# Norms' partition sums on GpSimd for three of four batches, in a fused attention and gated-FFN kernel

## The chip, the cores and the metric

One core of one Trainium2 chip. The metric is the device time of one execution in microseconds. All times below are medians of several executions.

## The reference

Four batches of cross-covariance attention over channels, and on its output a gated feed-forward block. N = 5824 rows, C = 256 channels, F = 1024.

```python
qn = q / (np.linalg.norm(q, axis=1, keepdims=True) + 1e-06)    # norms over the rows, one per channel
kn = k / (np.linalg.norm(k, axis=1, keepdims=True) + 1e-06)
s = kn.transpose(0, 2, 1) @ qn / tau                           # 256 x 256 per batch
s = s - s.max(-1, keepdims=True)
a = np.exp(s); a /= a.sum(-1, keepdims=True) + 1e-09
x = (v @ a).reshape(B * N, C)
out = ((x @ w1) * (x @ w2)) @ w3 @ w_out
```

## The kernel before

The kernel folds `a` into `w1` and `w2` (tiles `Wf`) and `w3 @ w_out` into `W_sb`. Each batch is then a long stream of steps: two products `a` and `b` from `vT` and `Wf` (TensorE), a cast `as` of `a` to bf16 (ScalarE), a product `abs` = `as` x `b` (VectorE), and the output product `o` (TensorE). Eight steps make a chunk of 512 rows, twelve chunks a batch; the last chunk of a batch is small, 192 rows. After each chunk `o` is copied out of PSUM (`osb`) by ScalarE and VectorE. The `a` and `b` products of all steps, and the row sums and folds too, rotate through four PSUM buffers with the tag `ab`:

```python
t = psum.tile([P, 512], F32, tag="ab", name=f"{'ab'[w]}_{b}_{c}_{j}", bufs=4)
...                                                       # 2 matmuls each
nc.scalar.copy(a_sb[:, :n], tiles[0][:, :n])              # the cast `as`
nc.vector.tensor_mul(ab, a_sb, tiles[1])                  # `abs`
```

While one batch streams, the softmax of the next one is prepared in between. Each engine's instructions run in the order in which they are issued here (below, casts stand 1.31 us behind exponentials that wait); an agenda of times (estimates of the program's own clock, not device times) decides where each piece falls:

```python
def norms():                                  # sums of squares of q and k, per partition
    a1 = work.tile([P, 2, C], F32, tag="acc1", ...)
    nc.vector.tensor_add(a1, accs[n][:, 0], accs[n][:, 1])
    st["ksq"] = a1[:, 1, :]; st["qsq"] = a1[:, 0, :]
def k_row():                                  # the chain: sum over partitions, then 1/(sqrt + eps)
    m = psum.tile([P, 512], F32, tag="ab", name=f"row_{n}", bufs=4)
    nc.tensor.matmul(m[:, :C], lhsT=ones_pp, rhs=st["ksq"], start=True, stop=True)
    nc.scalar.activation(out=kr, in_=m[:, :C], func=AF.Ln)
    ...                                       # three more on kr
def q_sums():
    ...                                       # two matmuls into ss_{n}, then q_norm: two small ScalarE, two small VectorE
def scaled():                                 # G is k^T q; s = G * kr on VectorE, then e = exp(s * r) on ScalarE
    for ct in range(CT): scale(ct)
    exps()
def sums(): ...                               # row sums of e on TensorE, into an "ab" buffer
...
head = [(0.0, norms), (0.5, k_row), (0.4, q_sums)]
return head + [(0.0, scaled), (0.2, sums)] + [(0.43, lambda i=i: fold(i)) for i in range(8)]
...
# times of: norms, k_row, q_sums, scaled, sums, then eight folds
ts = [t1 + 1.0, t1 + 3.5, t1 + 4.0, t1 + 8.0, t1 + 12.0] + [t1 + 13.0 + 0.9 * i for i in range(8)]
```

Of the kernel before, what the change touches and what calls it, by code (L numbers as in the profile page):

```python
# [7 lines left out]


# [1 line left out]
AF = mybir.ActivationFunctionType  # L11
ALU = mybir.AluOpType
F32 = DT.float32
# [11 lines left out]
def kernel(  # L25
# [213 lines left out]
    def soft_units(n):  # L239
        st = {}  # L240

        def k_first():
            d = work.tile([P, CT, P], F32, tag="sq", name="dk", bufs=2)
            nc.vector.tensor_mul(d, S["k"], ident.unsqueeze(1).to_broadcast([P, CT, P]))
            st["ksq"] = d.rearrange("p c t -> p (c t)")

        def q_first():
            d = work.tile([P, CT, P], F32, tag="sq", name="dq", bufs=2)
            ss = work.tile([P, CT], F32, tag="ss0", name="ss0", bufs=1)
            for ct in range(CT):  # L250
                nc.vector.tensor_tensor_reduce(
                    out=d[:, ct, :], in0=S["q"][:, ct, :], in1=ident, scale=1.0, scalar=0.0,
                    op0=ALU.mult, op1=ALU.add, accum_out=ss[:, ct : ct + 1],
                )
            st["ss"] = ss

        def scaled_first():
            scale(0)
            q_norm(st["ss"])
            scale(1)  # L260
            exps()

        def norms():
            a1 = work.tile([P, 2, C], F32, tag="acc1", name=f"acc1_{n}", bufs=1)
            nc.vector.tensor_add(a1, accs[n][:, 0], accs[n][:, 1])
            st["ksq"] = a1[:, 1, :]
            st["qsq"] = a1[:, 0, :]

        def k_row():

            m = psum.tile([P, 512], F32, tag="ab", name=f"row_{n}", bufs=4)
            nc.tensor.matmul(m[:, :C], lhsT=ones_pp, rhs=st["ksq"], start=True, stop=True)  # L272
            kr = work.tile([P, C], F32, tag="kr", name=f"kr_{n}", bufs=1)
            nc.scalar.activation(out=kr, in_=m[:, :C], func=AF.Ln)  # L274
            nc.scalar.activation(out=kr, in_=kr, func=AF.Exp, scale=0.5)
            nc.scalar.activation(out=kr, in_=kr, func=AF.Ln, bias=eps_t)  # L276
            nc.scalar.activation(out=kr, in_=kr, func=AF.Exp, scale=-1.0)
            st["kr"] = kr

        def q_sums():  # L280
            m = psum.tile([P, 512], F32, tag="ab", name=f"ss_{n}", bufs=4)
            for ct in range(CT):
                nc.tensor.matmul(
                    m[:, ct : ct + 1], lhsT=st["qsq"][:, ct * P : (ct + 1) * P], rhs=ones_f,
                    start=(ct == 0), stop=(ct == CT - 1), skip_group_check=True,
                )
            q_norm(m[:, :CT])

        def q_norm(src):
            r = work.tile([P, CT], F32, tag="r", name=f"r_{n}", bufs=2)  # L290
            nc.scalar.activation(out=r, in_=src, func=AF.Ln)
            nc.scalar.activation(out=r, in_=r, func=AF.Exp, scale=0.5)
            nc.vector.tensor_scalar_add(r, r, 1e-6)
            nc.vector.reciprocal(r, r)
            if inv_tau != 1.0:
                nc.vector.tensor_scalar_mul(r, r, inv_tau)
            st["r"] = r

        def scale(ct):
            if ct == 0:  # L300
                st["s"] = work.tile([P, CT, C], F32, tag="s", name=f"s_{n}", bufs=1)
            nc.vector.tensor_mul(st["s"][:, ct, :], G_tiles[n][:, ct, :], st["kr"])

        def exps():
            e = work.tile([P, CT, C], BF16, tag="e", name=f"e_{n}", bufs=2)
            for ct in range(CT):
                nc.scalar.activation(
                    out=e[:, ct, :], in_=st["s"][:, ct, :], func=AF.Exp, scale=st["r"][:, ct : ct + 1]
                )
            st["e"] = e  # L310

        def scaled():
            for ct in range(CT):
                scale(ct)
            exps()

        def sum_mm(c2):
            if c2 == 0:
                st["sum"] = psum.tile([P, 512], F32, tag="out" if n == 0 else "ab", name=f"sum_{n}", bufs=3 if n == 0 else 4)
                Wf[n] = wf_pool.tile([P, CT, 2, F], BF16, tag="Wf", name=f"Wf_{n}")  # L320
            m = st["sum"]
            for c1 in range(CT):
                nc.tensor.matmul(
                    m[:, c1 : c1 + 1], lhsT=st["e"][:, c2, c1 * P : (c1 + 1) * P], rhs=ones_b,
                    start=(c1 == 0 and c2 == 0), stop=(c1 == CT - 1 and c2 == CT - 1), skip_group_check=True,
                )
            if c2 == CT - 1:
                rs = work.tile([P, CT], F32, tag="rs", name=f"rs_{n}", bufs=2)
                nc.vector.tensor_scalar_add(rs, m[:, :CT], 1e-9)
                nc.vector.reciprocal(rs, rs)  # L330
                st["rs"] = rs

        def sums():
            sum_mm(0)
            sum_mm(1)

        def fold_mm(i, c2, tag="ab", on_act=None):
            h, rest = divmod(i, 4)
            w, c1 = divmod(rest, 2)
            if c2 == 0:  # L340
                st["fold", i] = psum.tile(
                    [P, 512], F32, tag=tag, name=f"fold_{n}_{i}", bufs={"ab": 4, "out": 3}[tag]
                )
            nc.tensor.matmul(  # L344
                st["fold", i], lhsT=st["e"][:, c2, c1 * P : (c1 + 1) * P], rhs=w12[:, c2, w, h * 512 : (h + 1) * 512],
                start=(c2 == 0), stop=(c2 == CT - 1),
            )
            if c2 == CT - 1:
                dst = Wf[n][:, c1, w, h * 512 : (h + 1) * 512]
                if on_act if on_act is not None else i % 2 == 0:  # L350
                    nc.scalar.activation(out=dst, in_=st["fold", i], func=AF.Copy, scale=st["rs"][:, c1 : c1 + 1])  # L351
                else:
                    nc.vector.tensor_scalar_mul(dst, st["fold", i], st["rs"][:, c1 : c1 + 1])

        def fold(i, tag="ab", on_act=None):
            fold_mm(i, 0, tag)
            fold_mm(i, 1, tag, i % 2 == 0 if on_act is None else on_act)

        def first_folds():
            sum_mm(0)  # L360
            fold_mm(0, 0)
            fold_mm(1, 0)
            sum_mm(1)
            fold_mm(0, 1)
            fold_mm(1, 1)
            fold(2)
            transpose_half_on_pe(0, 0, 0, False)
            fold(3, on_act=True)
            fold(4, "out", on_act=False)
            fold(5, "out")  # L370

        if n == 0:
            return [k_first, k_row, q_first, scaled_first, first_folds] + [lambda i=i: fold(i) for i in range(6, 8)]
        head = [(0.0, norms), (0.5, k_row), (0.4, q_sums)]
        return head + [(0.0, scaled), (0.2, sums)] + [(0.43, lambda i=i: fold(i)) for i in range(8)]


# [12 lines left out]
    def at(t, cost, fn):  # L390
        seq[0] += 1
        agenda.append((t, seq[0], cost, fn))
# [106 lines left out]
    busy(14)  # L499
    load_piece("k", 0, 0, (half,))  # L500
    load_piece("q", 0, 0, (half,))
    masks.make_identity(nc, ident)
    nc.vector.tensor_copy(ident_b, ident)
    w3_wout = vT_pool.tile([P, (NT - 1) * C], BF16, tag="vT", name="w3_wout")
    w3_bf = w3_wout[:, : FT * F].rearrange("p (j l) -> p j l", l=F)
    wout_sb = w3_wout[:, FT * F : FT * (F + D)].rearrange("p (l d) -> p l d", d=D)
# [2 lines left out]
    def transpose_w3():  # L509

        for h in range(FT // 2):
            m = in_pool.tile([P, 2, FT, P], BF16, tag="k", name=f"w3T_{h}", bufs=IN_BUFS["k"])
            nc.sync.dma_start_transpose(m, w3_bf[:, 2 * h : 2 * h + 2, :])
            w3T.append(m)

    w3r = moe_w3.rearrange("(jh jl) l -> jl jh l", jl=P)
    w1r = moe_w1.rearrange("(ch cl) f -> cl ch f", cl=P)
# [54 lines left out]
    def w_unit(jt):  # L572
# [10 lines left out]
        if jt == FT - 1:  # L583
            w_ready[0] = True


    def make_agenda(b):
        agenda.clear()
# [2 lines left out]
        if b == 0:  # L591
            for i in range(2):
                at(1.5 + 0.6 * i, 0.43, soft0[5 + i])
            at(4.0, 0.5, lambda: transpose_half_on_pe(0, 0, 1, False))
            at(7.0, 0.5, lambda: transpose_half_on_pe(0, 1, 0, True))
            at(8.0, 0.5, lambda: transpose_half_on_pe(0, 1, 1, False))
# [4 lines left out]
            moves = [("v", 0, 3, 29.0), ("qk", 1, 0, 38.0), ("qk", 1, 1, 43.0), ("v", 0, 4, 50.0), ("qk", 1, 2, 58.0)]  # L601
            moves += [("qk", 1, 3, 63.0), ("v", 0, 5, 70.0), ("qk", 1, 4, 81.0), ("qk", 1, 5, 87.0)]
            moves += [("v", 1, 0, 96.0), ("v", 1, 1, 106.0), ("v", 1, 2, 116.0), ("qk", 2, 0, 126.0)]
            t0, t1 = 58.0, 120.0
        else:
            moves = [("v", b, 3, 1.0), ("qk", n, 1, 10.0), ("qk", n, 2, 17.0), ("v", b, 4, 26.0), ("qk", n, 3, 38.0)]
            moves += [("v", b, 5, 46.0), ("qk", n, 4, 58.0), ("qk", n, 5, 66.0)]
# [20 lines left out]
        for i, (cst, fn) in enumerate(units):  # L628
            at(t0 + (t1 - t0) * i / len(units), cst, fn)
        soft = soft_units(n)  # L630
        ts = [t1 + 1.0, t1 + 3.5, t1 + 4.0, t1 + 8.0, t1 + 12.0] + [t1 + 13.0 + 0.9 * i for i in range(8)]
        for t, (cst, fn) in zip(ts, soft):
            at(t, cst, fn)
        agenda.sort()
# [50 lines left out]
```

## Time and profile before

| | before |
|---|---|
| time, median | 575.47 us in the runs given at the start; 575.46 to 575.79 in the rounds below |
| span of the profiled run | 573.6 us |
| TensorE busy | 561.9 us, 98% |
| next busiest: VectorE, ScalarE | 65%, 59% |

These are lines of the timeline of before around batch three's exponentials, ScalarE, then VectorE, then TensorE. Columns: start, duration, engine, line, operation, output<-inputs, shapes, count; in brackets the idle time just before it and what ended it.

```profile
295.28 0.58 ACT L431 CAST as<-a 128x512 bf16<-128x512 f32 x1 [0.35 <-PE a L425]
296.96 0.91 ACT L307 ACTIVATE e<-s,r 128x256 bf16<-128x256 f32 x2 [1.09 <-DVE s L302]
297.77 1.05 ACT L431 CAST as<-a 128x512 bf16<-128x512 f32 x2
...
296.50 0.75 DVE L302 TENSOR_TENSOR s<-G,kr 128x256 f32<-128x256 f32 x2
...
299.41 0.60 PE L466 MATMUL o<-W_sb,abs 128*128 128x256 bf16 x4
299.85 0.24 PE L323 MATMUL sum<-ones_b,e 128*128 128x1 bf16 x4
```

ScalarE already stands idle for 1.09 us here, with the exponentials at the head of its queue and casts behind them. TensorE does not notice: `sum` follows `o` without a bracket. How close that is can be worked out. TensorE starts an `a` every 1.30 us, so with four buffers for two products a step, the buffer of an `a` is wanted again two steps, 2.60 us, later. The first cast behind the exponentials serves the `a` that started at 295.95; its buffer is wanted at 298.55, and the cast, half of the 1.05 us from 297.77, ends at about 298.3. That leaves some 0.25 us.

### The profile page before, as it was taken

How to read it: one execution, taken by the hardware profiler on the slowest of the kernel's cores; microseconds unless marked ns; L12 is line 12 of the kernel's file. 1: busy time of each engine (PE TensorE's matmuls, PEld its weight loads, DVE VectorE, ACT ScalarE, POOL GpSimd, SP SyncE). 2: the span in 40 equal slices, each digit the busy share in tenths (PEclk: the TensorE clock that was granted, in tenths of full speed). 3: DMA queues.
4: the chain of work that ended last, by engine and by line, in shares of the span. 5: the costliest groups of instructions: out<-in, count | busy, mean ns of one | idle time of the engine just before them, and what ended most of it. 6: DMA issues, size and time to landing. Idle time of an engine off the chain costs nothing.

```text
span 573.6 us, 10125 instructions
## 1 busy us (share of the span) xinstructions
PE 561.9 (98%) x3760; PEld 357.0 (62%) x3766; DVE 374.1 (65%) x597; ACT 337.9 (59%) x624; POOL 71.0 (12%) x162
## 2 busy tenths in 40 slices
PE   8789999999999999999999999999999999999997
PEld 4755576776666666666666666666665666666665
DVE  0047744787967567887776567778876656565564
ACT  0046534777766567776765567767765555454453
POOL 5240020202010111221000012021100000000000
PEclk9999999999999999999999999999999999999999
DMA  8999959779574696495661596675740325221011
GB/s 163 211 194 208 188 99 235 175 171 213 134 185 108 123 207 151 95 190 120 147 147 49 117 192 143 132 142 119 184 110 38 85 74 146 63 63 74 38 71 59
DMA packets 74561, 76.93 MB, mean 134 GB/s; under 512 B 54161, under 2 KB 58257, under 8 KB 74513
## 3 DMA queue, kind: packets, MB, share of 16 engines
q0 software_dynamic: 15504, 39.46, 39.2%
q1 hardware_dynamic: 58784, 36.64, 21.1%
q8 instruction: 29, 0.48, 0.3%
q10 hardware_dynamic: 224, 0.20, 0.1%
q14 instruction: 20, 0.16, 0.1%
HBM read 78.91 MB, written 23.86 MB: 179 GB/s over the span
## 4 chain that ended last, share of the span: by engine, by line
PE 91%; DMA 5%; ACT 1%; issue 1%; DVE 1%; POOL 1%; ACTq 0%; POOLq 0%
PE o L466 27%; PE a L425 27%; PE b L425 27%; PE G L188 5%; DMA k<-in_k_dram 3%; PE fold L344 2%; DMA q<-in_q_dram 2%; PE w L575 1%; ACT as L431 1%; POOL k L109 0%; PE row L272 0%; POOL q L109 0%; DVE abs L440 0%; DVE osb L487 0%; ACT kr L276 0%
## 5 line engine op out<-in xcount | busy, mean ns | idle before, releaser
L440 DVE TENSOR_TENSOR abs<-as,b 128x512 bf16<-128x512 bf16 x336 | 229.7, 685 | 140.5 <-ACT as L431 128.7
L431 ACT CAST as<-a 128x512 bf16<-128x512 f32 (+1 forms) x384 | 215.4, 562 | 177.7 <-PE a L425 86.7
L425 PEld LDWEIGHTS <-Wf 128*128 128x128 bf16 x1536 | 149.1, 98 | 102.5 <-issue 2.6
L466 PE MATMUL o<-W_sb,abs 128*128 128x256 bf16 x1376 | 209.7, 273 | 0.5 <-ACT osb L486 0.4
L425 PE MATMUL a<-vT,Wf 128*128 128x512 bf16 x704 | 209.4, 379 | 0.4
L425 PE MATMUL b<-vT,Wf 128*128 128x512 bf16 x704 | 209.4, 379 | 0.0
L466 PEld LDWEIGHTS <-abs 128*128 128x128 bf16 x1376 | 134.5, 98 | 82.0 <-issue 0.6
L197 DVE TENSOR_TENSOR acc<-acc,sq 128x1024 f32<-128x1024 f32 x66 | 80.4, 1219 | 0.8 <-ACT sq L185 0.8
L188 PE MATMUL G<-k,q 128*128 128x256 bf16 x276 | 49.6, 273 | 0.0
L185 ACT ACTIVATE sq<-q 128x512 f32<-128x512 bf16 x66 | 41.8, 633 | 0.0
L185 ACT ACTIVATE sq<-k 128x512 f32<-128x512 bf16 x66 | 41.6, 630 | 0.0
L413 POOL COPY gate_t<-abs 1x1 bf16<-1x1 bf16 x39 | 12.1, 310 | 183.7 <-DVE abs L440 183.1
L487 DVE COPY osb<-o 128x512 f32<-128x512 f32 x44 | 30.1, 684 | 0.0
L188 PEld LDWEIGHTS <-q 128*128 128x128 bf16 x276 | 27.0, 98 | 3.1
L486 ACT COPY osb<-o 128x512 f32<-128x512 f32 x44 | 25.7, 585 | 4.6 <-PE o L466 2.6
L417 POOL COPY gate_t<-vT 1x1 bf16<-1x1 bf16 x17 | 4.0, 234 | 180.5 <-DMA vT<-v 145.1
L274 ACT ACTIVATE kr<-row 128x256 f32<-128x256 f32 x4 | 1.5, 384 | 34.0 <-PE row L272 34.0
L109 POOL DMA_DIRECT2D q<-in_q_dram x29 | 15.6, 538 | 12.5 <-DMA k<-in_k_dram 5.2
L344 PE MATMUL fold<-w,e 128*128 128x512 bf16 x61 | 16.5, 378 | 0.1
L351 ACT ACTIVATE Wf<-fold,rs 128x512 bf16<-128x512 f32 x16 | 10.9, 687 | 7.2 <-PE fold L344 4.3
L109 POOL DMA_DIRECT2D k<-in_k_dram x25 | 13.7, 550 | 3.9 <-DMA k<-in_k_dram 1.9
L109 POOL DMA_DIRECT2D v<-in_v_dram x25 | 13.4, 539 | 4.0 <-issue 2.6
(87 smaller groups left out, 219.1 us busy)
## 6 DMA issues: line engine op xcount, KB each, us to landing
out_dram<-osb SPq DMA_DIRECT2D x44, 512.0 KB, 3.1
k<-in_k_dram POOLq DMA_DIRECT2D x19, 512.0 KB, 8.8
v<-in_v_dram POOLq DMA_DIRECT2D x19, 512.0 KB, 5.1
q<-in_q_dram POOLq DMA_DIRECT2D x18, 512.0 KB, 6.5
w_wout<-in_moe_w_dram POOLq DMA_DIRECT2D x1, 2048.0 KB, 22.9
k<-in_k_dram POOLq DMA_DIRECT2D x4, 320.0 KB, 9.4
v<-in_v_dram POOLq DMA_DIRECT2D x4, 320.0 KB, 5.2
q<-in_q_dram POOLq DMA_DIRECT2D x4, 256.0 KB, 11.9
```

The source lines that it names most:

```text
L109: nc.gpsimd.dma_start(out=pieces[nm, n, pi][:, lo:hi, :], in_=qk_main[nm, n][0][:, pi * PIECE + lo : pi * PIECE + hi, :])
L185: nc.scalar.activation(out=dst[:, :, part, :], in_=src[:, o : o + 2, :], func=AF.Square)
L188: nc.tensor.matmul(G[:, ct, :], lhsT=qt[:, i, ct * P : (ct + 1) * P], rhs=kt[:, i, :], start=(pr == 0 and part == 0 and ct == 0), stop=(pr ...
L197: nc.vector.tensor_add(accs[n], accs[n], sqs[0])
L344: nc.tensor.matmul(st["fold", i], lhsT=st["e"][:, c2, c1 * P : (c1 + 1) * P], rhs=w12[:, c2, w, h * 512 : (h + 1) * 512], start=(c2 == 0), ...
L413: nc.gpsimd.tensor_copy(gate_t, last_ab[0][:1, :1])
L425: nc.tensor.matmul(t[:, :n], lhsT=Wf[b][:, ct, w, j * P : (j + 1) * P], rhs=rhs_of(b, c, ct), start=(ct == 0), stop=(ct == CT - 1),)
L431: nc.scalar.copy(a_sb[:, :n], tiles[0][:, :n])
L440: nc.vector.tensor_mul(ab, a_sb, tiles[1])
L466: nc.tensor.matmul(tl[h][:, o, :], lhsT=lhsT, rhs=W_sb[:, j, :], start=(j == 0 and o == 0), stop=(j == FT - 1 and (small or o == 1)), skip ...
L486: nc.scalar.copy(o[:, 0:2, :], tl[0])
L487: nc.vector.tensor_copy(o[:, 2:4, :], tl[1])
```

## The change

The intent: the sums over partitions leave TensorE, the bound engine. For batches two to four GpSimd does one all-reduce of 128x512 f32 (the squares of q and k together); the diagonal of the q half is taken with the identity on VectorE. The first GpSimd call of that kind, on one column, comes early so that its library is there. The agenda gives the all-reduce time by calling the chain later. The identity is no longer built on GpSimd, which frees that engine for loads at the start.

```diff
         def norms():
             ...
-            st["ksq"] = a1[:, 1, :]
-            st["qsq"] = a1[:, 0, :]
+            tot = work.tile([P, 2, C], F32, tag="s", name=f"tot_{n}", bufs=1)
+            nc.gpsimd.partition_all_reduce(tot..., a1..., P, ReduceOp.add)
+            st["tot"] = tot
         def k_row():
-            m = psum.tile([P, 512], F32, tag="ab", name=f"row_{n}", bufs=4)
-            nc.tensor.matmul(m[:, :C], lhsT=ones_pp, rhs=st["ksq"], start=True, stop=True)
+            if n == 0: ...                                # as before
+            else:
+                src = st["tot"][:, 1, :]
         def q_sums():
-            m = psum.tile([P, 512], F32, tag="ab", name=f"ss_{n}", bufs=4)
-            ...                                           # 2 matmuls
-            q_norm(m[:, :CT])
+            q_norm(diagonal(st["tot"][:, 0, :]...))       # 2 multiply-reduces with ident
...
-    masks.make_identity(nc, ident)
+    nc.vector.tensor_tensor_scan(idx, ones_pp, ones_pp, 0.0, ALU.mult, ALU.add)
+    nc.tensor.matmul(turned[:, :1], lhsT=idx[:1, :], rhs=ones_f[:1, :], start=True, stop=True)
+    ...
+    nc.vector.tensor_scalar(out=ident, in0=idx, scalar1=number, scalar2=None, op0=ALU.is_equal)
...
+            at(0.0, 0.0, load_library)                    # a 1-column all-reduce, behind the first loads
...
-            t0, t1 = 58.0, 120.0                          # first batch's stage only
+            t0, t1 = 57.0, 116.0
...
-        ts = [t1 + 1.0, t1 + 3.5, t1 + 4.0, t1 + 8.0, t1 + 12.0] + [t1 + 13.0 + 0.9 * i for i in range(8)]
+        late = 2.5 if b == 0 else 0.0
+        ts = [t1 + 1.0] + [t1 + late + t for t in (8.5, 9.0, 11.0, 14.5)] + [t1 + late + 15.5 + 0.9 * i for i in range(8)]
```

More of the change, by code (lines that the diff above doesn't have):

```diff
@@ L5 @@
 from concourse import bass_utils, mybir
-from concourse import masks
+from concourse.bass_isa import ReduceOp
 from concourse._compat import with_exitstack
@@ L245, in k_first @@
             st["ksq"] = d.rearrange("p c t -> p (c t)")
-        def q_first():
-            d = work.tile([P, CT, P], F32, tag="sq", name="dq", bufs=2)
-            ss = work.tile([P, CT], F32, tag="ss0", name="ss0", bufs=1)
-            for ct in range(CT):
-                nc.vector.tensor_tensor_reduce(
-                    out=d[:, ct, :], in0=S["q"][:, ct, :], in1=ident, scale=1.0, scalar=0.0,
-                    op0=ALU.mult, op1=ALU.add, accum_out=ss[:, ct : ct + 1],
-                )
-            st["ss"] = ss
         def scaled_first():
@@ L265, in norms @@
             nc.vector.tensor_add(a1, accs[n][:, 0], accs[n][:, 1])
-            st["ksq"] = a1[:, 1, :]
-            st["qsq"] = a1[:, 0, :]
-        def k_row():
-            m = psum.tile([P, 512], F32, tag="ab", name=f"row_{n}", bufs=4)
-            nc.tensor.matmul(m[:, :C], lhsT=ones_pp, rhs=st["ksq"], start=True, stop=True)
+            tot = work.tile([P, 2, C], F32, tag="s", name=f"tot_{n}", bufs=1)
+            nc.gpsimd.partition_all_reduce(
+                tot.rearrange("p w c -> p (w c)"), a1.rearrange("p w c -> p (w c)"), P, ReduceOp.add
+            )
+            st["tot"] = tot
+        def k_row():
+            if n == 0:
+                m = psum.tile([P, 512], F32, tag="ab", name=f"row_{n}", bufs=4)
+                nc.tensor.matmul(m[:, :C], lhsT=ones_pp, rhs=st["ksq"], start=True, stop=True)
+                src = m[:, :C]
+            else:
+                src = st["tot"][:, 1, :]
             kr = work.tile([P, C], F32, tag="kr", name=f"kr_{n}", bufs=1)
-            nc.scalar.activation(out=kr, in_=m[:, :C], func=AF.Ln)
+            nc.scalar.activation(out=kr, in_=src, func=AF.Ln)
             nc.scalar.activation(out=kr, in_=kr, func=AF.Exp, scale=0.5)
@@ L278, in k_row, with diagonal, q_first @@
             st["kr"] = kr
-        def q_sums():
-            m = psum.tile([P, 512], F32, tag="ab", name=f"ss_{n}", bufs=4)
-            for ct in range(CT):
-                nc.tensor.matmul(
-                    m[:, ct : ct + 1], lhsT=st["qsq"][:, ct * P : (ct + 1) * P], rhs=ones_f,
-                    start=(ct == 0), stop=(ct == CT - 1), skip_group_check=True,
-                )
-            q_norm(m[:, :CT])
+        def diagonal(src):
+            d = work.tile([P, CT, P], F32, tag="sq", name=f"dq_{n}", bufs=2)
+            ss = work.tile([P, CT], F32, tag="ss0", name=f"ss0_{n}", bufs=1)
+            for ct in range(CT):
+                nc.vector.tensor_tensor_reduce(
+                    out=d[:, ct, :], in0=src[:, ct, :], in1=ident, scale=1.0, scalar=0.0,
+                    op0=ALU.mult, op1=ALU.add, accum_out=ss[:, ct : ct + 1],
+                )
+            return ss
+        def q_first():
+            st["ss"] = diagonal(S["q"])
+        def q_sums():
+            q_norm(diagonal(st["tot"][:, 0, :].rearrange("p (c t) -> p c t", t=P)))
         def q_norm(src):
@@ L373, in soft_units @@
             return [k_first, k_row, q_first, scaled_first, first_folds] + [lambda i=i: fold(i) for i in range(6, 8)]
-        head = [(0.0, norms), (0.5, k_row), (0.4, q_sums)]
+        head = [(0.0, norms), (0.0, k_row), (0.0, q_sums)]
         return head + [(0.0, scaled), (0.2, sums)] + [(0.43, lambda i=i: fold(i)) for i in range(8)]
@@ L501 @@
     load_piece("q", 0, 0, (half,))
-    masks.make_identity(nc, ident)
-    nc.vector.tensor_copy(ident_b, ident)
     w3_wout = vT_pool.tile([P, (NT - 1) * C], BF16, tag="vT", name="w3_wout")
@@ L514, in transpose_w3 @@
             w3T.append(m)
+    idx = work.tile([P, P], F32, tag="sq", name="idx", bufs=2)
+    nc.vector.tensor_tensor_scan(idx, ones_pp, ones_pp, 0.0, ALU.mult, ALU.add)
+    turned = psum.tile([P, 512], F32, tag="ab", name="turned", bufs=4)
+    nc.tensor.matmul(turned[:, :1], lhsT=idx[:1, :], rhs=ones_f[:1, :], start=True, stop=True)
+    number = work.tile([P, 1], F32, tag="number", name="number", bufs=1)
+    nc.vector.tensor_copy(number, turned[:, :1])
+    nc.vector.tensor_scalar(out=ident, in0=idx, scalar1=number, scalar2=None, op0=ALU.is_equal)
+    nc.vector.tensor_copy(ident_b, ident)
     w3r = moe_w3.rearrange("(jh jl) l -> jl jh l", jl=P)
@@ L584, in w_unit, with load_library @@
             w_ready[0] = True
+    def load_library():
+        m = work.tile([P, 1], F32, tag="lib", name="lib", bufs=1)
+        nc.gpsimd.partition_all_reduce(m, ones_f, P, ReduceOp.add)
     def make_agenda(b):
```

## The prediction

> **What bounds the kernel now.** I read the page first (busy shares, then the chain of work that ended last), then who waits on TensorE, then three short stretches around the work that the change removes.
>
> ```profile
> PE 561.9 (98%) x3760; PEld 357.0 (62%) x3766; DVE 374.1 (65%) x597; ACT 337.9 (59%) x624; POOL 71.0 (12%) x162
> PE 91%; DMA 5%; ACT 1%; issue 1%; DVE 1%; POOL 1%; ACTq 0%; POOLq 0%
> ```
>
> TensorE is busy for 561.9 of 573.6 us, and 91% of the chain is TensorE; no other engine is above 65%. The waits on TensorE say the same from the other side:
>
> ```profile
> PE sqq L221 <- DMA q<-in_q_dram: 4.2, 4, 2.0
> PE warm_I-91_92 L209 <- DVE warm L78: 1.3, 1, 1.3
> PE sum L323 <- ACT e L307: 1.0, 1, 1.0
> PE o L466 <- ACT osb L486: 0.4, 1, 0.4
> PE sqk L221 <- DMA k<-in_k_dram: 0.2, 1, 0.2
> PE a L425 <- ACT as L431: 0.2, 1, 0.2
> ```
>
> All but the 0.4 and the 0.2 lie in the first 37 us, while batch one loads. After that the kernel is one unbroken stream of matmuls: an instruction taken out of that stream shortens the run by its start-to-start time, and an instruction on another engine is free unless TensorE comes to wait for it. What the change takes out (view of busy time by stretch; the columns are stretch, length, then busy time per engine with counts; each stretch runs from the start of the `row` matmul to the start of the next `a` matmul, as the timeline has them):
>
> ```profile
> 163.95:164.75 0.80, 0.80 (x8) 0.75 (x7) 0.64 (x1) 0.16 (x1) 0.00 (x0) 1.00 1.09 220
> 291.22:292.01 0.79, 0.79 (x8) 0.74 (x7) 0.64 (x1) 0.16 (x1) 0.03 (x1) 1.00 1.02 415
> 425.14:425.94 0.80, 0.80 (x9) 0.75 (x8) 0.64 (x1) 0.17 (x1) 0.00 (x0) 1.00 1.00 410
> ```
>
> The start of the kernel is bound by transfers, not by instructions. The same view:
>
> ```profile
> 3.00:4.00 1.00, 1.00 (x4) 0.39 (x3) 0.00 (x0) 0.00 (x0) 0.93 (x3) 1.00 0.72 102
> 4.00:5.00 1.00, 1.00 (x3) 0.30 (x2) 0.39 (x2) 0.00 (x0) 1.00 (x3) 1.00 1.08 201
> 5.00:6.00 1.00, 1.00 (x4) 0.38 (x3) 0.00 (x0) 0.00 (x0) 1.00 (x3) 1.00 1.12 209
> 10.00:15.00 5.00, 4.06 (x55) 3.44 (x54) 0.17 (x1) 0.00 (x0) 1.05 (x2) 1.00 1.05 211
> ```
>
> The last column is GB/s: some 205 from 4 us on. Batch one's q and k are 2 x 5824 x 256 x 2 bytes = 5.96 MB as stored; at 210 GB/s that is 28.4 us, and the last q piece releases TensorE at 32.66 us (chain of waits), so the transfers run without a hole.
>
> **What the Trainium skill says.** "Perfetto Trace Analysis", section "Tensor Engine Instruction (MATMUL, LD_WEIGHTS)": the reported end of a matmul is computed, not observed. The trace agrees: the matmuls of `row` show 0.60 us from 163.95 and those of `ss` 0.50 us, together 1.10, yet the next stream starts 0.80 us after `row`. So I use start-to-start times and not the 1.8 + 1.5 us of busy time in the list of groups, which would overstate the gain by about a third. "GPSIMD Engine Reference", "2.1 Instruction dispatch": the first call into a freshly loaded library costs about 6 us and no instruction shows it; no run here shows that yet. The same page, "3.2 Cross-partition — where GPSIMD wins": a partition-axis tensor_reduce of [128, 2048] took 247,699 ns. It is another instruction than this all-reduce, and the trace of before has neither. "SBUF — State Buffer", "Who interferes with whom": GpSimd shares its port pair with VectorE, as an exclusive lock. The VectorE work with two SBUF inputs is the adding of squares (1219 ns each), and the last of those comes before the all-reduce, which needs their sum. What then lies beside it reads one operand from PSUM.
>
> **The change, part by part.**
>
> 1. Three `row` matmuls and six `ss` matmuls leave TensorE (each f32 one is two passes in the trace). Worth 0.80 + 0.79 + 0.80 = 2.39 us, all on the path, since TensorE has no hole there. Batch one's `row` stays.
>
> 2. In batch two the chain of logarithms and exponentials on ScalarE moves. Before, it ran from 164.59 to 166.61 (0.38 + 0.42 + 0.51 + 0.42, and two small ones), just ahead of an `osb` copy, and TensorE waited 0.39 us for that copy; this is the 0.4 of the list of waits. In the changed order the copy stands two casts before the chain. That wait should go: 0.39 us. In batches three and four the chain now stands two casts ahead of an `osb` copy, one step of 1.30 us earlier relative to it than the arrangement that cost 0.39, so I expect no wait there.
>
> 3. Three all-reduces of 128x512 f32 come onto GpSimd, which is 12% busy. Their length is the unknown. The change gives each 7.5 us in its schedule between the sum of squares and the ScalarE chain (times +1.0 and +8.5), and 10 us in batch two. What that is worth on the chip I read from before. Batch three: the sum of squares ended at 290.4 us on VectorE, and the next ScalarE cast (the fourth of that chunk) stood at 290.55; in the changed order the chain follows the eighth cast of the chunk, four steps of 1.30 us and one cast later, so at about 296.2: 5.8 us. Batch two: GpSimd stands behind a v load, issued at 161.11 and done at 161.64 before, and the chain follows a cast three steps after the one that ended at about 163.8, so at 167.7: 6.0 us. If it ends inside that, it costs nothing. A spacing that comes out so alike in two batches, by a special allowance in one, looks measured and not guessed.
>
> 4. VectorE gets, per batch, two multiply-reduces with the identity and two accumulator reads; batch one shows their cost, 288 + 82 ns, so 0.74 us a batch. VectorE is at 65%: free.
>
> 5. The identity: GpSimd loses a memset and an affine select between the first loads and the second k piece (that load starts at 4.02 us and could start at 3.45, 0.57 us earlier). The chain of waits of before runs through exactly these instructions, and a naive reading would book 0.57 us. The rates say no: data move at 201 to 209 GB/s from 4 us on, when that load has only just been issued, so transfers are already queued without a hole. I book 0. In exchange come a scan and one small matmul at about 7 us, before the first squares; TensorE waits 4.2 us for q later in that stage, so they are absorbed.
>
> 6. The library load stands after the last weight load. GpSimd is idle from 37.2 to 72.5 us there, 35 us for an estimated 6. Free.
>
> 7. In batch one's main stage the scores are packed into 59 us of schedule instead of 62. That moves the first use of the fifth k piece from 141.40 to about 138.8 us (16 matmuls earlier), while that piece was issued at 129.86 and took 9.2 us: it would be late by some tenths. But in the new order the transposes of the last v piece, whose landing at 128.6 us released that load, stand one output transfer earlier in the SyncE queue, so the load should leave several us earlier. I book 0.
>
> Sum: 575.47 - 2.39 - 0.39 = 572.7. With 0.1 for small new waits: 572.8 us, 0.5% less.
>
> **The rivals.**
>
> A. The all-reduce outlasts its slot and a ScalarE wait takes the matmul's place. ScalarE works in order, so its casts stop too, and TensorE with four `ab` buffers can run ahead by about one step (1.3 us) before it stops. An excess of 2 us would cost some 0.7 x 3 = 2 us and eat the gain: 575. At the skill's figure for the tensor_reduce, scaled to 512 columns (an estimate: 62 us), it would be 55 x 3 = 165 us: about 738. For it: the skill's number. Against: it is another instruction, and the spacing of 7.5 us.
>
> B. The moved ScalarE chain collides with an `osb` copy or with the folds, which now come later and in batch two all stand among the small last chunk. Up to 0.4 us a batch, as the one case shows: 574.0. Against: a small step there is 0.77 us plus 0.43 for a fold, and ScalarE needs about 0.3 plus every second time 0.7.
>
> C. The head does gain from the earlier second k load: 572.2. Against: the rates above.
>
> D. A late k piece in batch one's stage (part 7 fails): up to 1 us, 573.8.
>
> E. The library load holds GpSimd beyond 35 us: v piece 3 comes late and the run gets longer by the excess. Nothing in the profile speaks for it.
>
> **Range and chances.** The removed matmuls are nearly certain; C pulls to 572.2, B and D push towards 574, a mild A to 575. The three runs of before spread over 0.64 us. So 571.7 to 574.4 for eight in ten. Faster by over 2% would need 11.5 us, which nothing offers: 0.01. Slower by over 2% is only strong A or E: 0.04. Within 2%: 0.95.
>
> **What would show it.** TensorE's matmul count falls by what `row` and `ss` had, and the list of waits has no wait of TensorE on `osb` at 167 us. Part 3: the first instruction of the chain on ScalarE is released by ScalarE's own queue or has under 1 us idle before it, not a long wait on GpSimd; idle of more than about 1.5 us there is rival A. Part 5: the first `fold` of batch one starts within 0.2 us of 37.07. Part 6: the GpSimd copy that stood at 72.54 is no later. Part 7: no wait of TensorE or ScalarE on the fifth k piece near 139 us. I am wrong in kind if the run is not faster at all, and most likely then through A.

## The result, and the profile after

The changed kernel takes 575.19 us (574.94 to 575.28, 4 runs), before 575.55 us (575.47 to 576.11, 4 runs). The ratio is 0.9991, 95% interval 0.9974 to 1.0008: no difference that these runs resolve. A ratio here and below is the mean time of one kernel's runs over that of the other's of the same rounds, so not quite the ratio of the medians quoted. The predicted 572.8 us, and its range up to 574.4, were missed on the slow side.

The page after, engines and chain:

```profile
PE 559.5 (98%) x3744; PEld 354.8 (62%) x3750; DVE 377.3 (66%) x612; ACT 337.4 (59%) x624; POOL 82.9 (14%) x164
PE 86%; DMA 6%; ACT 4%; DVE 2%; issue 1%; POOL 1%; ACTq 0%; DVEq 0%; POOLq 0%
```

TensorE has 16 matmuls fewer in the records, 2.4 us less busy time, and yet the span is 573.5 us as against 573.6. So TensorE idles more, and ScalarE and VectorE now hold 4% and 2% of the chain where they had 1% each. TensorE's waits after (total us, times, longest):

```profile
PE sum L327 <- ACT as L435: 1.6, 2, 0.8
...
PE a L429 <- ACT as L435: 0.7, 3, 0.2
...
PE b L429 <- ACT as L435: 0.2, 1, 0.2
```

The wait on `osb` that the prediction wanted gone is gone. In its place stand waits for a cast `as`, above all in front of `sum`, in two batches. Busy time in the stretch from 290 to 312 us, which holds batch three's softmax, before and then after (stretch, length, then busy time of TensorE, its loads, VectorE, ScalarE, GpSimd with counts; clock, DMA share, GB/s):

```profile
290.00:312.00 22.00, 21.82 (x135) 12.83 (x134) 14.17 (x26) 13.30 (x26) 1.41 (x4) 1.00 0.39 96
```

```profile
290.00:312.00 22.00, 20.88 (x129) 12.26 (x129) 14.14 (x30) 13.29 (x27) 4.54 (x5) 1.00 0.39 96
```

TensorE is idle 1.12 us of this stretch after the change and 0.18 before; ScalarE and VectorE do the same amount of work in both. The timeline after shows where the idle time lies; ScalarE, VectorE, TensorE around the same exponentials:

```profile
298.94 0.60 ACT L490 COPY osb<-o 128x512 f32<-128x512 f32 x1
300.85 0.91 ACT L311 ACTIVATE e<-s,r 128x256 bf16<-128x256 f32 x2 [1.31 <-DVE s L306]
301.66 1.05 ACT L435 CAST as<-a 128x512 bf16<-128x512 f32 x2
...
299.80 0.68 DVE L491 COPY osb<-o 128x512 f32<-128x512 f32 x1
300.40 0.74 DVE L306 TENSOR_TENSOR s<-G,kr 128x256 f32<-128x256 f32 x2
...
298.69 0.59 PE L429 MATMUL a<-vT,Wf 128*128 128x512 bf16 x2
...
300.85 0.60 PE L470 MATMUL o<-W_sb,abs 128*128 128x256 bf16 x4
302.27 0.24 PE L327 MATMUL sum<-ones_b,e 128*128 128x1 bf16 x4 [0.82 <-ACT as L435]
302.76 0.59 PE L429 MATMUL a<-vT,Wf 128*128 128x512 bf16 x2 [0.25 <-ACT as L435]
```

The exponentials stand at the head of ScalarE's queue and wait 1.31 us for `s`. The first cast behind them serves the `a` that started at 298.69. By the rule above its buffer is wanted at 301.29; the cast ends at about 302.2. TensorE's next user of that buffer, `sum`, starts at 302.27, 0.98 us late. (The bracket says 0.82 because the end of a matmul is modelled; I count from start to start.) A second gap of 0.38 us follows behind `sum`. Before, the same cast had 0.25 us to spare.

Three ledgers tell where the 2.4 us went. Start times of the same cast of the 384, after minus before: -0.33 us when batch two's stream starts, -0.26 when batch three's starts, -0.18 when batch four's starts, and -0.18 at the end. So batches three and four gain nothing: the 0.79 and 0.80 us removed are given back. Second, TensorE's gaps between matmul starts beyond those of an unbroken stream, leaving out one-matmul holes that look like missing records, in batch three's softmax stage: 0.52 us before, 1.37 after, so 0.85 more; the same in batch four, 0.51 and 1.37. Third, before batch two's stream: the wait on `osb` went, but 0.39 and 0.32 us (from start to start) appeared in front of an `a` and a `b`, of the same sort:

```profile
173.67 0.33 PE L429 MATMUL a<-vTt,Wf 128*128 128x192 bf16 x2 [0.22 <-ACT as L435]
174.16 0.32 PE L429 MATMUL b<-vTt,Wf 128*128 128x192 bf16 x2 [0.16 <-ACT as L435]
```

The start-up of the profiled run was 0.23 us slower, measured at a cast of the fourth chunk; among the other kernels that figure runs from -0.2 to +0.6.

The part that was expected to be risky is quiet. GpSimd's all-reduce of batch two, and the head of the ScalarE chain that uses it:

```profile
162.54 3.19 POOL L257 PARTITION_ALL_REDUCE tot<-acc  x1
...
167.90 0.42 ACT L271 ACTIVATE kr<-tot 128x256 f32<-128x256 f32 x1
```

It takes 3.19 us (3.23 in the other two batches), ends at 165.7, and the chain starts at 167.90 with no bracket: no wait for GpSimd. VectorE's products beside it take what they take elsewhere: `abs` has a mean of 686 ns in this run and 685 before.

### The profile page after: what moved, and what is told of

Read it like the earlier page. It is cut to its first block, busy times and chain, and to the rows that moved or that the text cites. A ratio compares the mean times of both kernels' runs of the same rounds, so it can differ in the third digit from the quotient of the medians.

```text
span 573.5 us, 10096 instructions
## 1 busy us (share of the span) xinstructions
PE 559.5 (98%) x3744; PEld 354.8 (62%) x3750; DVE 377.3 (66%) x612; ACT 337.4 (59%) x624; POOL 82.9 (14%) x164
## 4 chain that ended last, share of the span: by engine, by line
PE 86%; DMA 6%; ACT 4%; DVE 2%; issue 1%; POOL 1%; ACTq 0%; DVEq 0%; POOLq 0%
PE o L470 26%; PE a L429 26%; PE b L429 26%; PE G L188 5%; DMA k<-in_k_dram 5%; PE fold L348 2%; ACT as L435 2%; DVE abs L444 1%; DMA w<-in_moe_w_dram 1%; PE w L587 1%; ACT e L311 0%; POOL k L109 0%; ACT kr L273 0%; POOL q L109 0%; DVE osb L491 0%
## 5 line engine op out<-in xcount | busy, mean ns | idle before, releaser
L417 POOL COPY gate_t<-abs 1x1 bf16<-1x1 bf16 x39 | 13.8, 354 | 168.8 <-DVE abs L444 167.9
```

The lines of the kernel that those rows point to most:

```text
L417: nc.gpsimd.tensor_copy(gate_t, last_ab[0][:1, :1])
```

## The experiments

The theory after reading the result: the removal is worth what was predicted, and the new spacing of the agenda gives it back through ScalarE's queue. Rivals: the all-reduce on GpSimd slows VectorE or ScalarE; the new identity or the library call cost time; the exponentials merely are too close to the row sums. Unless said otherwise an edit is against the changed kernel. All twelve were timed in five rounds (four to six executions each) beside runs of the kernel before on the same chip. None of the twelve differs from it by 2%; where a gain or a loss is claimed, the interval of its ratio leaves out 1.

### e5: the removal alone, wrong result

Before, with the `row` and `ss` matmuls of batches two to four left out; ScalarE reads the unsummed squares instead, so the result is wrong, the timing is not.

```diff
-            nc.tensor.matmul(m[:, :C], lhsT=ones_pp, rhs=st["ksq"], start=True, stop=True)
+                src = st["ksq"]                       # batches two to four
...
-            ...                                       # the two ss matmuls
-            q_norm(m[:, :CT])
+            q_norm(st["qsq"][:, :CT])
```

> Wrong result on purpose. The kernel before, its own schedule, with the row and ss matmuls of batches two to four left out and nothing in their place (the ScalarE chain reads the unsummed squares), so neither GpSimd nor the new spacing is in it. It measures by itself what leaving TensorE is worth. If the stream theory holds (2.39 us removed, and TensorE finds no new wait): 575.6 - 2.4 = 573.2 us; if the 0.39 us wait on the osb copy goes too, 572.8; if the matmuls had been partly hidden, above 574.

Measured: 573.38 us against 575.79, ratio 0.9959 (0.9947 to 0.9972). The 2.4 us are real and lie on the path. Something in the change gives them back.

### e3: the new spacing alone

Before, with its matmuls, under the changed agenda.

```diff
-        head = [(0.0, norms), (0.5, k_row), (0.4, q_sums)]
+        head = [(0.0, norms), (0.0, k_row), (0.0, q_sums)]
...
-            t0, t1 = 58.0, 120.0
+            t0, t1 = 57.0, 116.0
...                                                   # and the changed kernel's `late` and `ts`
```

> The kernel before (matmuls for the norms, old identity, no GpSimd work) with the changed kernel's schedule: the same times and the same order of instructions on ScalarE as the changed kernel. Spacing theory: the loss comes without any all-reduce, so the kernel before gets slower by what the change lost: 575.5 + 0.9 + 0.9 + 0.2 = about 577.4 us (576.8 to 578). GpSimd theory: the loss needs the all-reduce, so 575.5 us.

Measured: 577.64 us against 575.63, ratio 1.0047 (1.0026 to 1.0069). Five executions lie between 577.52 and 578.04; one at 582.07 stands apart, and is counted in the ratio. TensorE's waits hold the same line as in the changed kernel:

```profile
PE sum L323 <- ACT as L431: 1.5, 2, 0.7
```

No all-reduce runs here, and the loss is there, 2.0 us. So GpSimd is not needed to explain it; the agenda is. With e5 the account closes: 2.41 us for the removal less 2.01 for the spacing leave 0.40, and the change as a whole gained 0.36.

### e4: the new identity alone

Before, with only the identity from a scan and one matmul.

```diff
-    masks.make_identity(nc, ident)
+    nc.vector.tensor_tensor_scan(idx, ones_pp, ones_pp, 0.0, ALU.mult, ALU.add)
+    ...                                               # as in the change
```

> The kernel before with only the identity changed (scan, one small matmul, compare on VectorE; nothing on GpSimd between the first loads). The changed kernel reached its first a matmul 0.37 us later than the kernel before (0.23 us from chunk three on). If the identity is the cause, this kernel is 0.2 to 0.4 us slower, 575.8 us; if it is chance in the loads or the library load, 575.5 us within 0.2. A reader of the chain of waits would have said 0.57 us faster, 574.9.

Measured: 575.49 us against 575.63, ratio 0.9997 (0.9985 to 1.0009). No effect that these runs resolve.

### e7: the library not brought in early

```diff
-            at(0.0, 0.0, load_library)
```

> The changed kernel without the small all-reduce that brings the library in; it is then brought in by batch two's own all-reduce, while ScalarE's chain is due 2.1 us after that ended in the changed kernel. With the skill's 6 us for a first call the chain starts about 4 us late, TensorE hides about 1.3 of it: 575.2 + 2.7 = about 578 us. If the load is short or runs ahead, 575.2 us, and bringing it in early bought nothing.

Measured: 575.30 us, ratio 0.9993 (0.9979 to 1.0007): as the changed kernel. Batch two's all-reduce is then the first of its kind, and it starts almost at once:

```profile
162.81 3.19 POOL L257 PARTITION_ALL_REDUCE tot<-acc  x1 [0.20 <-DVE abs L444]
```

The miss: no 6 us appear. The start is 0.27 us later than with the early call, in a run whose casts there are some tenths later too (while batch one loaded, TensorE idled 2.23 us in it and the clock then read 0.50 from 20.50 to 23.91 us), and the length is the same 3.19 us. The early call buys nothing that can be measured here.

### e6: the old spacing, with the all-reduce

```diff
-            t0, t1 = 57.0, 116.0
+            t0, t1 = 58.0, 120.0
...
-        ts = [t1 + 1.0] + [t1 + late + t for t in (8.5, 9.0, 11.0, 14.5)] + [...]
+        ts = [t1 + 1.0, t1 + 3.5, t1 + 4.0, t1 + 8.0, t1 + 12.0] + [t1 + 13.0 + 0.9 * i for i in range(8)]
```

> The changed kernel with the whole schedule of the kernel before (scores to 120, chain 2.5 us after the sum of squares, scaling 4.0 after the q sums, sums 4.0 after that). The all-reduce takes 3.2 us, and the chain is due some 1.4 us after the sum of squares ends, so ScalarE waits about 1.9 us three times (in batch two longer, for GpSimd is at the v load). TensorE can run ahead about one step of 1.3 us. So rival A made real: 573.2 plus some 0.6 to 1.5 us a batch, 575 to 577 us. If TensorE runs further ahead than I think, 573.5, and the change's later chain was not needed.

Measured: 583.98 us (583.45 to 585.48), ratio 1.0148 (1.0134 to 1.0162). The direction was expected, the size was not. ScalarE's chain, TensorE's restart, and one stretch behind it (the clock is the third number from the end):

```profile
297.82 0.42 ACT L271 ACTIVATE kr<-tot 128x256 f32<-128x256 f32 x1 [2.68 <-POOL tot L257]
...
300.53 1.01 PE L429 MATMUL a<-vT,Wf 128*128 128x512 bf16 x2 [2.54 <-ACT as L435]
...
301.00:302.00 1.00, 1.00 (x4) 0.36 (x3) 0.79 (x2) 0.42 (x1) 0.00 (x0) 0.50 1.02 205
```

ScalarE waits 2.68 us for the all-reduce, TensorE idles 2.54, and then its clock is granted at 0.50 for about 3 us. The same happens in batch two, after 2.83 us; in batch four TensorE idles 2.55 us without a drop of the clock. So the change did need a later chain. What it did not need is what it did with the exponentials.

### e1: exponentials, sums and folds later

In batches three and four the distance from the chain to `scaled` grows from 2.5 to 4.5, and the sums and folds move by 2.5.

```diff
+        wide = 0.0 if b == 0 else 2.0
-        ... (8.5, 9.0, 11.0, 14.5)] + [t1 + late + 15.5 + 0.9 * i for i in range(8)]
+        ... (8.5, 9.0, 11.0 + wide, 14.5 + 1.25 * wide)] + [t1 + late + 15.5 + 1.25 * wide + 0.9 * i for i in range(8)]
```

> The changed kernel with the softmax stage of batches three and four spread as it was before: the scaling of G 4.0 us of schedule after the q sums (not 2.0) and the column sums and folds 2.5 us later; batch two as it is. My theory now (spacing: ScalarE stands still at the exponentials e, because VectorE delivers s late, and TensorE then waits at sum): the excess over an unbroken matmul stream in those two batches falls from about 1.4 us each to about 0.5, so 575.2 - 1.7 = 573.5 us. Rival (the all-reduce on GpSimd slows VectorE or ScalarE): nothing moves, 575.2 us, within 0.3.

Measured: 573.89 us (573.69 to 574.17) against 575.63, ratio 0.9969 (0.9957 to 0.9981). The wait of `sum` for a cast is gone from the list. It falls some tenths short of 573.5: a gap of 0.28 us and one of 0.06 stay in each of the two batches, since `s` has moved too and ScalarE still waits 1.42 us for it. The folds, now later, also run into the small last chunk: in batch three gaps of 0.17 and 0.21 us appear there at 313 us, which the changed kernel does not have.

### e2: the chain earlier

```diff
-        ... (8.5, 9.0, 11.0, 14.5)] ...
+        ... (6.5, 7.0, 11.0, 14.5)] ...
```

> The changed kernel with only the norms' ScalarE chain and the q sums 2.0 us of schedule earlier, in all three batches; scaling, sums and folds stay where the change has them. The all-reduce took 3.2 us, so it still ends first. Spacing theory: r and the scaling get their 4 us back, so TensorE's wait at sum goes: about 573.5 us (573.2 to 574.2). Rival (GpSimd): 575.2 us. If it were only the distance between scaling and sums that counts, 575.2 as well while the wider kernel gains.

Measured: 575.12 us against 575.63, ratio 0.9990 (0.9977 to 1.0003). A miss: the wait only moved. The chain's own last part and TensorE, in batch three:

```profile
297.50 0.20 ACT L295 ACTIVATE r<-ss 128x2 f32<-128x2 f32 x1 [1.18 <-DVE ss L281]
...
298.46 0.59 PE L429 MATMUL a<-vT,Wf 128*128 128x512 bf16 x2 [0.34 <-ACT as L435]
```

Now ScalarE waits 1.18 us for `ss`, with casts behind it again, and TensorE waits 0.50 us there (start to start), and again 0.38 before and 0.38 behind the sums. At this point two readings fitted e1 and e2: distance between scaling and sums, or the order of ScalarE's queue. The last four runs tell them apart.

### e8: the wide spacing in every batch

```diff
-        ... [t1 + late + t for t in (8.5, 9.0, 11.0, 14.5)] + [t1 + late + 15.5 + 0.9 * i ...]
+        ... [t1 + t for t in (8.5, 9.0, 13.0, 17.0)] + [t1 + 18.0 + 0.9 * i ...]     # and one v load of batch two at 120.0, not 116.0
```

> Meant as the better version: the wider spacing in all three batches, and in batch two the all-reduce ahead of the last v load instead of behind it, so that it needs no extra 2.5 us. Against the wider kernel with batch two untouched (573.89 us) it takes away the 0.79 us of wait that TensorE has at 173.1 to 174.3 us on ScalarE's casts behind the exponentials: 573.2 us. If the small last chunk simply hands the wait on to the folds: 573.9.

Measured: 573.69 us (573.42 to 575.13) against 575.79, ratio 0.9970 (0.9958 to 0.9983). As e1; in batch two the gap merely changed its place (0.58 us in front of an `a` at 168.36).

### e9: sums and folds later, exponentials where they were

```diff
+        far = 0.0 if b == 0 else 2.5
-        ... 14.5)] + [t1 + late + 15.5 + 0.9 * i ...]
+        ... 14.5 + far)] + [t1 + late + 15.5 + far + 0.9 * i ...]
```

> Changed kernel, but in batches three and four the row sums and folds come 2.5 us later; the chain, the scaling and the exponentials stay where they were. Two readings of where the gain went. (A) Distance: the exponentials are merely not ready when the row sums come, so more room between scaling and sums is all that is needed; then this run does as the wider spacing did, 573.8 us. (B) Head of line: the exponentials stand in ScalarE's queue ahead of two casts and wait there for VectorE's scaling; the casts hold the four buffers of TensorE's a and b products, so whatever matmul comes next for a buffer (the sums before, now an a product) waits as long. Then ScalarE's wait of 1.3 us for s stays, TensorE's 0.8 us wait moves from the sums to an a product, and only the shorter wait behind the sums (0.38 us) can go: 574.6 to 575.2.

Measured: 574.98 us (574.79 to 575.38) against 575.48, ratio 0.9992 (0.9979 to 1.0004). So the reading by distance falls. ScalarE and TensorE in batch three:

```profile
300.46 0.91 ACT L311 ACTIVATE e<-s,r 128x256 bf16<-128x256 f32 x2 [1.31 <-DVE s L306]
...
301.89 0.59 PE L429 MATMUL a<-vT,Wf 128*128 128x512 bf16 x2 [0.82 <-ACT as L435]
```

The two brackets are those of the changed kernel to the hundredth, 1.31 and 0.82. Only the waiting instruction is another: an `a` stands where `sum` stood. The gap behind the sums goes, but the later folds cost some 0.4 us in batch three's small last chunk, as in e1.

### e10: exponentials one cast later, nothing else

`scaled` is split in batches three and four; the scaling stays, the exponentials come 1.5 later, which puts exactly one cast ahead of them.

```diff
-        return head + [(0.0, scaled), (0.2, sums)] + ...
+        return head + [(0.0, scales), (0.0, exps), (0.2, sums)] + ...
...
-        ... (8.5, 9.0, 11.0, 14.5)] ...
+        ... (8.5, 9.0, 11.0, 11.0 if b == 0 else 12.5, 14.5)] ...
```

> Changed kernel, but in batches three and four the two exponentials are put one cast later in ScalarE's queue (1.5 us later), nothing else. (B) Head of line: the cast that frees the buffer is done before the exponentials, so ScalarE's wait for s shrinks from 1.3 us to about 0.6 or less and TensorE's wait at the sums from 0.98 to about 0.5 (the sums then wait for the exponentials themselves, about 0.5 us earlier than the cast came): 0.5 us or a little more a batch, 574.0 us (573.6 to 574.4). (A) Distance: the exponentials come later while the sums stay, so the sums wait as long or longer: 575.2 or more.

Measured: 573.17 us (573.02 to 573.38) against 575.48, ratio 0.9959 (0.9947 to 0.9972). Better than expected. ScalarE, then TensorE, in batch three:

```profile
299.02 0.61 ACT L439 CAST as<-a 128x512 bf16<-128x512 f32 x1
300.45 0.91 ACT L311 ACTIVATE e<-s,r 128x256 bf16<-128x256 f32 x2 [0.82 <-DVE s L306]
...
301.01 0.20 PE L331 MATMUL sum<-ones_b,e 128*128 128x1 bf16 x2
301.41 0.20 PE L331 MATMUL sum<-ones_b,e 128*128 128x1 bf16 x2 [0.20 <-ACT e L311]
```

The exponentials start at the same 300.45, since `s` sets their start. But the cast at 299.02 is done before them and the buffer comes free in time. The gaps fall from 1.37 to 0.45 us a batch, so 0.91 us saved in each; I had expected 0.5, because I had not counted that the second gap, behind `sum`, goes with the first. Twice 0.91 is 1.8 of the 2.2 us by which this run's last casts precede the changed kernel's; the rest, about 0.4, is start-up difference between the runs (0.39 at the cast of the fourth chunk).

### e11: both

```diff
+        far = 0.0 if b == 0 else 2.5
+        ... (8.5, 9.0, 11.0, 11.0 + 0.6 * far, 14.5 + far)] + [t1 + late + 15.5 + far + 0.9 * i ...]   # with the split of e10
```

> Changed kernel with both: exponentials one cast later in ScalarE's queue, row sums and folds 2.5 us later, in batches three and four; the chain and the scaling stay. (B) Head of line: no wait of TensorE for a cast at the sums or at an a product is left in these batches, beyond what the kernel before had: 573.6 us (573.3 to 573.9), about 0.8 us a batch below the changed kernel. (A) Distance alone: same as the run with the sums alone later, whatever that gives.

Measured: 573.31 us (573.16 to 574.17) against 575.48, ratio 0.9968 (0.9954 to 0.9982). No wait for a cast is left at the sums, as expected, and later sums add nothing on balance to the reordered exponentials: the gaps at the sums fall to 0.07 us a batch (0.45 in e10), but the folds that moved with them bring 0.17 and 0.21 us in batch three's small last chunk.

### e12: exponentials one cast later in batch two as well

```diff
-        ... (8.5, 9.0, 11.0, 11.0 if b == 0 else 12.5, 14.5)] ...
+        ... (8.5, 9.0, 11.0, 12.5, 14.5)] ...
```

> The previous edit, exponentials one cast later in ScalarE's queue, now in batch two as well. The head-of-line reading says: in batch two ScalarE waits 1.20 us for s with three casts behind the exponentials, and TensorE waits 0.39 and 0.32 us at an a and a b product of the last chunk; with one cast ahead of the exponentials both go, or shrink to under 0.2 together: 0.5 to 0.7 us less than the run without it (573.17), 572.6 us (572.2 to 573.0), ratio to before 0.995. If those two waits in batch two have another cause (the small last chunk itself, the output copy), nothing changes: 573.2.

Measured: 572.56 us (572.41 to 573.13) against 575.46, ratio 0.9951 (0.9938 to 0.9965). Batch two, ScalarE, then TensorE where the changed kernel had waited 0.39 and 0.32 us:

```profile
171.90 0.91 ACT L311 ACTIVATE e<-s,r 128x256 bf16<-128x256 f32 x2 [0.34 <-DVE s L306]
...
172.93 0.33 PE L433 MATMUL a<-vTt,Wf 128*128 128x192 bf16 x2
173.10 0.33 PE L433 MATMUL b<-vTt,Wf 128*128 128x192 bf16 x2
```

Both waits are gone, a gap of 0.23 us behind the row sums is new; batch two's stream starts 0.51 us earlier than in e10. This is the fastest correct version, 0.5% below before and about as much as was once predicted for the change.

## Why the prediction was wrong, point by point

- **Part 1, the removed matmuls: right.** 2.39 us expected, 2.4 measured in e5.
- **Part 2, the moved ScalarE chain: the step that failed.** For batch two it said of the wait on `osb`, "That wait should go: 0.39 us". It went, but 0.39 and 0.32 us came in its place six microseconds later. For batches three and four it said the chain stands ahead of an `osb` copy "so I expect no wait there". There is no wait on `osb` there, but there were 0.85 us more of gaps in each. The sum had 0.1 us for small new waits; they came to 2.4, 0.7 in batch two and 1.7 in the other two. I had asked only how the four long instructions of the chain lie against the output copy. I had not asked what the last two of ScalarE's softmax instructions, the exponentials, lie against. In the agenda before, `scaled` comes 4.5 after the chain, three casts; in the changed one 2.5, two casts. So one cast more stands behind exponentials that wait for `s`, and the 0.25 us to spare becomes 0.98 late. e9 and e10 settle this: moving the sums leaves the loss, moving the exponentials by one cast takes it away. Both figures were in the diff, 8.0 - 3.5 and 11.0 - 8.5. Why ScalarE waits for `s` a little longer than before (1.31 against 1.09) is argued only: VectorE's own `osb` copy of 0.68 us now stands right before the scaling, and no run takes it away.
- **Part 3, the all-reduce fits its slot: right.** The estimates were slots of 5.8 and 6.0 us; it takes 3.2, and no ScalarE instruction waits for it in the changed kernel. e6 shows how dear it would have been in the old place.
- **Part 4, VectorE's extra work is free, and part 5, the identity: right.** VectorE's busy time rose by 3.2 us without a wait of TensorE on it, and e4 reads 0.9997. The first `fold` stands at 37.10 us, within the 0.2 us of 37.07 that was asked for.
- **Part 6, the library: right that it is free**, though its test as written failed: the GpSimd copy named there came at 72.99 us instead of 72.54. Its release was a transposed v piece, while the library call had ended at 37.65.
- **Part 7, no late k piece: right.** That pair of loads was issued from 127.90 us on instead of 129.34, and no wait stands near 139.
- **Rival A, named as the likeliest way to be wrong, did not happen. Rival B came nearest:** the moved group does collide on ScalarE, but with neither of the two things it named, output copy or folds. "Up to 0.4 us a batch" was taken from a collision with an output copy; the loss in batches three and four was 0.85, through the exponentials. The sum with measured terms: 575.5 - 2.4 (matmuls) - 0.4 (`osb`) + 0.7 (batch two's new gaps) + 1.7 (batches three and four) = 575.1, and 575.19 was measured.

## What to carry to other kernels

When work leaves the bound engine and a schedule is shifted to make room, check every instruction of the shifted group on each in-order queue: what it waits for, and which buffer releases stand behind it. An instruction that comes early and waits is not harmless; it delays all that is queued behind it, and with a ring of buffers the time to spare is one turn of the ring (here 2.60 us) less the delay. Moving the waiting instruction behind one buffer release was worth 0.9 us a batch here, while giving its consumer more distance was worth nothing on balance, since the folds that moved with it met the small last chunk.

## What the Trainium skill lacked or had wrong

- "GPSIMD Engine Reference", section "2.1 Instruction dispatch", gives about 6 us extra for the first call into a fresh library. With the early call left out (e7), batch two's first all-reduce started 0.20 us after GpSimd fell idle, took the same 3.19 us as with it, and the time was 575.30 against 575.19 us. The trace does show a switch there: two MODIFY_POOL_CONFIG records at 162.68 and 162.71 us, the only ones of that execution, 0.13 us before the all-reduce starts at 162.81. Nothing of 6 us shows. Whether a library stays loaded from one execution to the next was not tested.
- The same page, section "3.2 Cross-partition — where GPSIMD wins", has 247,699 ns for a partition-axis tensor_reduce of [128, 2048] and no figure for the all-reduce used here: 3.19 to 3.23 us for 128x512 f32, 0.40 us for one column. These are the profile's durations, which are rough on GpSimd; in e6, where ScalarE waits for the all-reduce, the two agree: it starts at 294.56 us and its first user at 297.82.
- "TensorE: Matmul & The Clock Gate", section "What's actually happening", puts the fall to half clock after an idle window of about 3.4 us. Here shorter idle times were enough, but not always: the clock read 0.50 for about 3 us after TensorE had idled 2.83 us (e6, batch two), 2.54 us (e6, batch three) and 2.23 us (e7, while batch one loaded), and did not fall after 2.55 us (e6, batch four). So the length of the idle time alone does not decide it; what does was not tested.
